# A two-stage transformer block: rows for the gMLP turned on VectorE instead of TensorE, the first w_in pieces made on GpSimd, and four accumulators instead of three and an auxiliary one

## The chip, the cores and the metric

The kernel runs as one program on one core of a Trainium2 chip. The metric is the device time of one execution in microseconds (us); the number that counts is the median of several executions. Five engines work side by side, each through its own list of instructions in order: TensorE (PE in the profile, with its weight loads as PEld), VectorE (DVE), ScalarE (ACT), GpSimd (POOL), and SyncE (SP), which in this kernel does nothing but issue DMAs. Sixteen DMA engines carry the transfers.

## What is computed

S = 2048 tokens of width D = 640. First an attention layer over a sliding window of 256 tokens with 32 heads, then a gated MLP that mixes tokens (gMLP), each behind a layer norm and with a residual:

```python
h  = x + A(layernorm(x))                      # attention, ends in o @ wo
z  = gelu(layernorm(h) @ w_in)                # w_in: 640 x 1728
z1, z2 = z[:, :864], layernorm(z[:, 864:])
g  = w_sp @ z2 + b_sp                         # mixes the 2048 tokens
out = h + (z1 * g) @ w_out
```

All products are made in pieces: every float32 operand is split into a high and a low part, and three products (high high, high low, low high) replace one. Some products also use a seven-product scheme for 2 by 2 blocks, which needs sums and differences of blocks of the operands ("pieces" below).

## The kernel before

The program runs in stages: attention (until about 465 us of the profile), the output projection with the residual and the second layer norm (about 465 to 547 us), the product with the first half of w_in (the z stage, about 547 to 640 us), and then the second half of w_in, the token mixing and the last product. The change lies in the projection stage and at its border to the z stage.

The projection stage goes over 16 tiles of 128 tokens (the loop at L1325). For tile i:

- `norm_o` (L166, DVE) multiplies the attention output, which DMAs have brought in turned form (L150, and L156 for the reciprocal sums), by those sums; `split_o` makes its high part (L174, ACT) and low part (L175, DVE). Both run ahead of TensorE by one to three tiles.
- `proj_o` makes 30 products of 128x320 (L96) into an accumulator of two PSUM banks. There are three accumulators (L703).
- DVE adds the residual and takes the row sum in one instruction (L1345), which also frees the accumulator; ACT squares (L1348), DVE and POOL make the factor of the layer norm (L1347, L1350, a power on POOL at L1351, L1355), and ACT writes the normalised row hn(i), 128 tokens by 640 (L1356).
- `turn_h` (L847 to L858) turns hn(i - 3): five TensorE transposes of 128x128 (L856) into an auxiliary PSUM tile of two banks (there is one, L706), an ACT copy (L723) into one of three SBUF buffers `ho`, and one DMA that stores it to `hn_d` in HBM, 128 runs of 2560 bytes. The last three tiles are turned while the z stage has begun, through other PSUM banks.

In the same stage `win1_prep` (L776) prepares the first half of w_in for the z stage: 16 weight tiles `zl`, each with a high part (ACT, L732 and L799) and a low part (a subtraction of 128x432), and 8 differences of blocks; the 24 subtractions all run on DVE (they pass through the helper at L717, as most additions and subtractions do).

The z stage (`z_pair`, L872) takes two tiles at a time, 8 pairs: it loads the two turned rows from `hn_d` (L889, L890) into the buffer `fx`, which also holds some of the rows hn(i) before they are turned, makes pieces of them on ACT and DVE (L717, L723), and multiplies (L916). Later `z2_pair` loads the same rows again (L977).

The order of instructions on each engine is set by a scheduler in this part of the program; each engine then keeps that order strictly. So an instruction that waits holds up all that stand behind it on its engine, and on SP a DMA that waits for its data holds up all DMAs behind it.

Of the kernel before, what the change touches and what calls it, by code (L numbers as in the profile page):

```python
# [15 lines left out]
P = 128  # L16
S = 2048
D = 640
# [16 lines left out]
def block_kernel(ctx, tc, x, wqk, wv, wo, w_in, wsp, bsp, w_out, out):  # L35
# [16 lines left out]
    r_d = dram.tile([H, S], F32, name="r_d")  # L52
    h_d = dram.tile([NT, P, D], F32, name="h_d")
    z1_d = dram.tile([NT, P, FH], F32, name="z1_d")
    hn_d = dram.tile([NT, P, D], F32, name="hn_d")
    g_d = dram.tile([NT, P, FH], F32, name="g_d")
    wo_d = dram.tile([KD, P, D], F32, name="wo_d")
    z2_d = dram.tile([2, P, FH], F32, name="z2_d")
# [660 lines left out]
    def minus(out, a, b, eng=None):  # L719
        plus(out, a, b, OP.subtract, eng)  # L720

    def copy(out, a):
        nc.scalar.activation(out, a, AF.Copy)  # L723

    B11, T1, T2, B22, T3, B21, T4 = range(7)

    def right_blocks(pieces, b11, b12, b21, b22, eng=None, one=1.0):

        raw = {B11: b11, T1: b11, T2: b11, B22: b22, T3: b12, B21: b21, T4: b21}

        def hi(m):
            nc.scalar.activation(pieces()[m][:, 0], raw[m], AF.Copy, scale=one)  # L732

        def lo(m, e=None):
            minus(pieces()[m][:, 1], raw[m], pieces()[m][:, 0].bitcast(F32), e)

        def second():
            lo(B11)
            minus(b11, b12, b11)
            hi(T1)  # L740

        def fourth():
            hi(B22)
            minus(b11, b22, b11)
# [31 lines left out]
    def win1_prep(raw):  # L776
        seven, last = win1
        rest = [r.rearrange("p (h c) -> p h c", h=2) for r in rows[2:]]

        def pieces(k, blocks, one):  # L780
            return right_blocks(lambda: [s[k] for s in seven], *(b[:, h] for b in blocks for h in range(2)), one=one)

        yield
        for n, f in enumerate(pieces(0, [raw[:, b] for b in range(2)], 1.0)):
            f()
            if n == 2:
                for b in range(2):
                    nc.sync.dma_start(rows[2 + b], w_in[(2 * b + 1) * P:(2 * b + 2) * P, :FH])
            yield
        nc.sync.dma_start(raw[:, 0], w_in[4 * P:, :FH].rearrange("k (h c) -> k h c", h=2))  # L790
        yield
        yield
        for f in pieces(1, rest, ones[:, 0:1]):
            f()
            yield
        yield
        for j in range(2):
            hi, lo = two(last[j])
            nc.scalar.activation(hi, raw[:, 0, j], AF.Copy, scale=ones[:, 1:2])  # L799
            minus(lo, raw[:, 0, j], hi.bitcast(F32))  # L800
        yield

    def win2_prep(raw):
# [42 lines left out]

    def turn_h(i):  # L847
        ht = mem["ho"][i % 3]
        if i < NT - 3:
            ps = aux_tile(f"ht_ps{i}").rearrange("p a b -> p (a b)")  # L850
            parts = [(0, KD, ps)]
        else:
            parts = [(0, 4, bank("b", f"ht_a{i}")), (4, KD, bank("b", f"ht_b{i}"))]
        for k0, k1, ps in parts:
            for k in range(k0, k1):
                nc.tensor.transpose(ps[:, (k - k0) * P:(k - k0 + 1) * P], hn(i)[:, k * P:(k + 1) * P], ident)  # L856
            copy(ht[:, k0 * P:k1 * P], ps[:, :(k1 - k0) * P])
        nc.sync.dma_start(hn_d[i], ht)  # L858


    steps, later = [], {}
# [10 lines left out]
    def z_pair(q, i, j, w):  # L872
# [76 lines left out]
    def z2_pair(q, i, j, k, ahead=False):  # L949
# [24 lines left out]
        for t, tile_t in ((0, i), (1, j)):  # L974
            m = n0 + 2 * t
            soon = q == 13
            at(m - (5 if soon else 12 if q == 8 else 6), lambda t=t, tile_t=tile_t: nc.sync.dma_start(r[t], hn_d[tile_t]))  # L977
# [347 lines left out]
    for i in range(NT):  # L1325
        if 1 < i + 1 < NT:
            split_o(i + 1, i == 1)
        if i % 2 == 0 and i + 6 < NT:
            for f in load_o(i // 2 + 3)[:2]:
                f()  # L1330
        if i + 2 < NT:
            norm_o(i + 2, nc.vector)
        for n in (4,) if i == 0 else (i + 4,) if i + 4 < NT else ():
            load_x2(n)
        run(i - NT)
        if i < 2:
# [8 lines left out]
        nc.vector.tensor_tensor_reduce(out=h3, in0=ps[:, :, :HD], in1=h3, scale=1.0, scalar=0.0,  # L1345
                                       op0=OP.add, op1=OP.add, accum_out=mv[:, 0:1])
        nc.vector.tensor_scalar(out=mv[:, 1:2], in0=mv[:, 0:1], scalar1=-1.0 / D, scalar2=None, op0=OP.mult)  # L1347
        nc.scalar.activation(hn(i), xt, AF.Square, bias=mv[:, 1:2], accum_out=mv[:, 2:3])  # L1348
        nc.scalar.dma_start(h_d[i], xt)
        nc.vector.tensor_scalar(out=mv[:, 2:3], in0=mv[:, 2:3], scalar1=1.0 / D, scalar2=EPS, op0=OP.mult, op1=OP.add)  # L1350
        nc.gpsimd.tensor_tensor(out=mv[:, 3:4], in0=mv[:, 2:3], in1=half, op=OP.pow)  # L1351
# [4 lines left out]
        nc.scalar.activation(hn(i), xt, AF.Identity, scale=mv[:, 3:4], bias=mv[:, 4:5])  # L1356
        next(w1, None)
        if i % 2:
            next(w1, None)
    for _ in w1:  # L1360
        pass
    w2p = None
    for n in range(len(steps)):
        run(n)
        if n < 3:
            turn_h(NT - 3 + n)
        if n == 2:
            open_d()
            w2p = win2_prep(view(fx, 4 * D + 256, FH))
        if n > 2:  # L1370
            next(w2p, None)
# [36 lines left out]
```

## Time and profile before

| | us |
|---|---|
| median of 3 runs | 1111.28 (1109.02 to 1111.66) |
| span of the profiled execution | 1108.2 |
| what lies between that span and the median | 3.1 |
| TensorE busy in that span | 1084.3 |
| VectorE, ScalarE, GpSimd busy | 720.7, 571.0, 369.6 |

Times in the profile count from the start of the span, and a line number L856 is line 856 of the kernel before. Busy TensorE time is modelled from overlapping instructions, so the distance between the starts of two neighbours is the better measure of what one costs; the same holds on the other engines for short instructions. DMA shares are the mean busy share of the 16 DMA engines.

### The profile page before, as it was taken

How to read it: one execution, taken by the hardware profiler on the slowest of the kernel's cores; microseconds unless marked ns; L12 is line 12 of the kernel's file. 1: busy time of each engine (PE TensorE's matmuls, PEld its weight loads, DVE VectorE, ACT ScalarE, POOL GpSimd, SP SyncE). 2: the span in 40 equal slices, each digit the busy share in tenths (PEclk: the TensorE clock that was granted, in tenths of full speed). 3: DMA queues.
4: the chain of work that ended last, by engine and by line, in shares of the span. 5: the costliest groups of instructions: out<-in, count | busy, mean ns of one | idle time of the engine just before them, and what ended most of it. 6: DMA issues, size and time to landing. Idle time of an engine off the chain costs nothing.

```text
span 1108.2 us, 27795 instructions
## 1 busy us (share of the span) xinstructions
PE 1084.3 (98%) x10667; PEld 974.4 (88%) x10667; DVE 720.7 (65%) x2043; ACT 571.0 (52%) x1215; POOL 369.6 (33%) x524
## 2 busy tenths in 40 slices
PE   9999999999999999989999999999999999999998
PEld 7998877668888877788899999999999999999998
DVE  6541212879999998677567478676637985566543
ACT  4333433249999999567776567433326531122210
POOL 3114444457777778512100055256422000000000
PEclk9999999999999999999999999999999999999999
DMA  7212565565666654678755421447593663444321
GB/s 261 74 35 96 166 221 179 196 210 181 214 204 214 215 177 120 193 254 281 242 188 193 151 80 39 165 154 233 190 339 113 204 215 114 129 132 150 100 91 65
DMA packets 88501, 187.80 MB, mean 169 GB/s; under 512 B 11648, under 2 KB 48144, under 8 KB 84448
## 3 DMA queue, kind: packets, MB, share of 16 engines
q1 hardware_dynamic: 83728, 172.08, 47.8%
q0 software_dynamic: 2336, 8.70, 2.2%
q10 hardware_dynamic: 2304, 5.24, 1.2%
q8 instruction: 84, 1.38, 0.5%
q14 instruction: 49, 0.40, 0.1%
HBM read 121.66 MB, written 65.52 MB: 169 GB/s over the span
## 4 chain that ended last, share of the span: by engine, by line
PE 78%; DMA 8%; DVE 3%; issue 3%; POOL 3%; ACT 3%; SPq 2%; ACTq 0%; POOLq 0%; DVEq 0%
PE g L1165 20%; PE zb L968 9%; PE out_ps L1218 8%; PE pv L435 6%; PE bank L341 5%; PE bank L407 5%; PE zx L916 3%; PE zv L916 2%; PE qk L525 2%; PE qk L526 2%; PE qk L527 2%; DMA qk_d<-sg 2%; PE zy L916 2%; SPq L320 1%; PE zw L916 1%
## 5 line engine op out<-in xcount | busy, mean ns | idle before, releaser
L410 ACT ACTIVATE pt<-bank 128x384 f32<-128x384 f32 (+2 forms) x512 | 200.8, 496 | 10.4 <-PE bank L407 5.7
L1165 PE MATMUL g<-zl,aw 128*128 128x432 f32 x768 | 169.7, 359 | 0.0
L353 DVE CUSTOM_DVE_ANT_0 junk<-bank,strip 128x288 bf16<-128x288 f32 x392 | 157.7, 454 | 4.3 <-PE bank L341 3.0
L723 ACT ACTIVATE aw<-fx 128x512 fp32r<-128x512 f32 (+2 forms) x147 | 84.9, 592 | 141.1 <-PE g L1165 101.9
L1165 PEld LDWEIGHTS g<-zl,aw 128*128 128x128 f32 x768 | 143.5, 188 | 6.1
L1165 PE MATMUL g<-ze,aw 128*128 128x432 f32 x576 | 131.9, 359 | 1.1 <-DVE row L717 1.1
L435 PE MATMUL pv<-pt,v_sb 128*32 128x192 f32 (+3 forms) x1984 | 127.3, 323 | 3.8 <-POOL pt L415 1.3
L717 DVE TENSOR_TENSOR aw<-fx,aw 128x512 fp32r<-128x512 f32 (+2 forms) x146 | 99.4, 690 | 28.6 <-ACT aw L723 23.5
L1165 PEld LDWEIGHTS g<-ze,aw 128*128 128x128 f32 x576 | 107.1, 188 | 6.2 <-DVE row L717 1.8
L407 PE MATMUL bank<-slot 123*32 123x288 bf16 (+5 forms) x1536 | 106.1, 282 | 1.0 <-ACT pt L410 0.4
L412 POOL TENSOR_SCALAR_AFFINE_SELECT pt<-pt 128x512 f32<-128x512 f32 x128 | 82.9, 648 | 43.6 <-ACT pt L410 42.4
L1218 PE MATMUL out_ps<-wout,y_sp 128*128 128x320 f32 (+1 forms) x630 | 96.4, 309 | 0.4 <-ACT y_sp L137 0.4
L968 PE MATMUL zb<-win,aw 128*128 128x432 f32 x480 | 95.0, 359 | 0.5 <-ACT aw L723 0.5
L1218 PEld LDWEIGHTS out_ps<-wout,y_sp 128*128 128x128 f32 (+1 forms) x630 | 94.2, 188 | 1.0 <-ACT y_sp L137 0.7
L968 PEld LDWEIGHTS zb<-win,aw 128*128 128x128 f32 x480 | 90.1, 188 | 5.0 <-ACT aw L723 0.9
L341 PE MATMUL bank<-slot 120*32 120x288 bf16 (+2 forms) x1264 | 89.8, 285 | 1.1 <-DVE mcol L353 1.0
L541 DVE TENSOR_TENSOR rest<-qk,sg 128x512 f32<-128x512 f32 x40 | 27.7, 692 | 86.1 <-ACT sg L539 86.1
L415 POOL TENSOR_SCALAR_AFFINE_SELECT pt<-pt 128x512 f32<-128x512 f32 x112 | 74.6, 666 | 0.0
L717 DVE TENSOR_TENSOR row<-g,row 128x432 f32<-128x432 f32 x80 | 48.2, 603 | 33.8 <-PE g L1165 30.3
L544 POOL TENSOR_TENSOR sg<-rest,sg 128x512 bf16<-128x512 f32 x40 | 46.6, 1166 | 69.2 <-ACT sg L543 60.2
L435 PEld LDWEIGHTS pv<-pt,v_sb 128*32 128x32 f32 x1984 | 59.5, 110 | 10.3 <-POOL pt L415 3.2
L407 PEld LDWEIGHTS <-slot 123*32 123x32 bf16 x1536 | 52.6, 96 | 16.2 <-issue 5.0
(216 smaller groups left out, 2195.1 us busy)
## 6 DMA issues: line engine op xcount, KB each, us to landing
fx<-wsp_in SPq DMA_DIRECT2D x30, 512.0 KB
slot<-qk_d SPq DMA_DIRECT2D x72, 200.0 KB
qk_d<-sg SPq DMA_DIRECT2D x32, 384.0 KB
slot<-qk_d SPq DMA_DIRECT2D x72, 160.0 KB
fx<-hn_d SPq DMA_DIRECT2D x32, 320.0 KB
o_d<-ot SPq DMA_DIRECT2D x64, 128.0 KB
z_d<-row SPq DMA_DIRECT2D x18, 432.0 KB
g_d<-row SPq DMA_DIRECT2D x16, 432.0 KB
```

The lines of the kernel that those rows point to most:

```text
L341: nc.tensor.matmul(ps[32 * j:32 * j + 32, :n], part(st, half, 120, 0, hh, q0, 32), part(st, half, 120, 1, hh, lo + skip * j, n), start=Tru ...
L353: nc.vector.tensor_tensor_reduce(out=junk[:, :n], in0=ps[:, :n], in1=keep, scale=1.0, scalar=NEG, op0=OP.add, op1=OP.max, accum_out=m_cols ...
L407: nc.tensor.matmul(ps[32 * i:32 * i + 32, b:e], part(st, half, 123, 1, hh, k0, 32), part(st, half, 123, 0, hh, kb * P + b, e - b), start=T ...
L410: nc.scalar.activation(pt[:, hh, :n], ps[:, :n], AF.Exp, scale=SCALE)
L412: nc.gpsimd.affine_select(out=pt[:, :, :P], in_=pt[:, :, :P], pattern=[[0, 4], [1, P]], base=0, channel_multiplier=-1, compare_op=OP.is_ge ...
L435: nc.tensor.matmul(ps[32 * hh:32 * hh + 32, a - 512 * c:b - 512 * c], v_sb[:, kb, v0:v0 + 32], pt[:, hh, a - kb * P:b - kb * P], start=fir ...
L717: (eng or nc.vector).tensor_tensor(out=out, in0=a, in1=b, op=op)
L723: nc.scalar.activation(out, a, AF.Copy)
L916: nc.tensor.matmul(ps, a[x], b[:, y], start=start and m + x + y == 0, stop=stop and m == n - 1 and x == 1, skip_group_check=True)
L968: nc.tensor.matmul(b[0][:, :HF], a[t][:, x, kk], win2[0][:, y, kk, h * HF:(h + 1) * HF], start=kk + x + y == 0, stop=kk == KD - 1 and x == 1)
L1165: nc.tensor.matmul(ps, w[m][x][:, k], zc[k][m][:, y], start=start and k + x + y == 0, stop=stop and k == 3 and x == 1, skip_group_check=True)
L1218: nc.tensor.matmul(ps[j][:, :HD], src[:w, a, k, :], e1["wout"][:w, b, k, j * HD:(j + 1) * HD], start=(k == 0 and a + b == 0), stop=(k == K ...
```

## The change

1. `turn_h` no longer uses TensorE. VectorE transposes the 128x640 row in blocks of 32x32 from SBUF to SBUF (one instruction), and four DMAs on SP put the blocks where a full transpose would have put them: DMA number a takes the 32 partitions from 32a on and stores 32 x 20 runs of 32 floats (128 bytes). Five transposes and one copy (two copies for the last three tiles) per tile go, one VectorE instruction and three more DMAs per tile come. In `hn_d` the 640 features now stand in another order, which is the same for every tile: the rows of `w_in` are reordered on the host to match.
2. `turn_h(i - 1)` is called at the end of iteration i, instead of `turn_h(i - 3)` in the middle of it; the last tile is turned at the first step of the z stage.
3. All 24 subtractions of `win1_prep` go to GpSimd.
4. The auxiliary PSUM tile goes, and there are four accumulators instead of three.

```diff
-    hn_d = dram.tile([NT, P, D], F32, name="hn_d")
+    hn_d = dram.tile([NT, 32, 4 * D], F32, name="hn_d")
...
-        return pools["c"].tile([P, 2, 512], F32, tag="acc", bufs=3, name=name)
-
-    def aux_tile(name):
-        return pools["c"].tile([P, 2, 512], F32, tag="aux", bufs=1, name=name)
+        return pools["c"].tile([P, 2, 512], F32, tag="acc", bufs=4, name=name)
...
         def pieces(k, blocks, one):
-            return right_blocks(lambda: [s[k] for s in seven], *(b[:, h] for b in blocks for h in range(2)), one=one)
+            return right_blocks(lambda: [s[k] for s in seven], *(b[:, h] for b in blocks for h in range(2)),
+                                nc.gpsimd, one, nc.gpsimd)
...
-            minus(lo, raw[:, 0, j], hi.bitcast(F32))
+            minus(lo, raw[:, 0, j], hi.bitcast(F32), nc.gpsimd)
...
     def turn_h(i):
         ht = mem["ho"][i % 3]
-        if i < NT - 3:
-            ps = aux_tile(f"ht_ps{i}").rearrange("p a b -> p (a b)")
-            parts = [(0, KD, ps)]
-        else:
-            parts = [(0, 4, bank("b", f"ht_a{i}")), (4, KD, bank("b", f"ht_b{i}"))]
-        for k0, k1, ps in parts:
-            for k in range(k0, k1):
-                nc.tensor.transpose(ps[:, (k - k0) * P:(k - k0 + 1) * P], hn(i)[:, k * P:(k + 1) * P], ident)
-            copy(ht[:, k0 * P:k1 * P], ps[:, :(k1 - k0) * P])
-        nc.sync.dma_start(hn_d[i], ht)
+        nc.vector.transpose(ht, hn(i))
+        dst = hn_d[i].rearrange("i (c a j) -> a i c j", a=4, j=32)
+        for a in range(4):
+            nc.sync.dma_start(dst[a], ht[32 * a:32 * a + 32].rearrange("i (c j) -> i c j", j=32))
+
+    def hn_rows(i):
+        return hn_d[i].rearrange("i (b c) -> b i c", b=4)
...
-            nc.sync.dma_start(ri, hn_d[i])
-            nc.sync.dma_start(rj, hn_d[j])
+            nc.sync.dma_start(ri, hn_rows(i))
+            nc.sync.dma_start(rj, hn_rows(j))
...
-        if i > 2:
-            turn_h(i - 3)
...
+        if i:
+            turn_h(i - 1)
...
-        if n < 3:
-            turn_h(NT - 3 + n)
+        if n == 0:
+            turn_h(NT - 1)
...
+    w_in = np.asarray(B_w_in).reshape(4, KD, 32, 2 * FH).transpose(1, 0, 2, 3).reshape(D, 2 * FH)
```

The scheduler makes a new order from this, in the projection stage and the z stage. In the rows below the lines of the changed kernel are 7 lower than those of the kernel before from L1345 on (L1338 is L1345, L1343 is L1350, L1348 is L1355), and L717 has become L714. A number behind `xh`, `mvc`, `ho` and `wo_ps` is that of the tile or buffer; `xb` holds the split attention output.

VectorE between the accumulator reads of tile 2 and tile 3, before:

```order
L1345 ISA xh2_8952,mvc2_9703<-wo_ps2_9672,xh2_8952 128x640
L1345 ISA mvc2_9703 128x1
L1350 TENSOR_SCALAR mvc1_9649<-mvc1_9649 128x1
L175 TENSOR_TENSOR xb1_100<-m1_8949,xb0_99 128x640
L717 TENSOR_TENSOR zl2_9603<-wraw_8956,zl2_9603 128x432
L1345 ISA xh3_8953,mvc3_9758<-wo_ps3_9719,xh3_8953 128x640
L1345 ISA mvc3_9758 128x1
L166 TENSOR_TENSOR m1_8949<-m1_8949 128x5x128 x2
L1347 TENSOR_SCALAR mvc2_9703<-mvc2_9703 128x1
L175 TENSOR_TENSOR xb0_99<-m1_8949,xb0_99 128x640
```

and at the same place now:

```order
L1338 ISA xh2_8952,mvc2_9708<-wo_ps2_9677,xh2_8952 128x640
L1338 ISA mvc2_9708 128x1
L1343 TENSOR_SCALAR mvc1_9649<-mvc1_9649 128x1
L847 STREAM_TRANSPOSE ho0_9595<-row0_9617 128x640
L175 TENSOR_TENSOR xb1_100<-m1_8949,xb0_99 128x640
L1340 TENSOR_SCALAR mvc2_9708<-mvc2_9708 128x1
L1338 ISA xh3_8953,mvc3_9760<-wo_ps3_9729,xh3_8953 128x640
L1338 ISA mvc3_9760 128x1
L175 TENSOR_TENSOR xb0_99<-m1_8949,xb0_99 128x640
L1348 TENSOR_TENSOR mvc1_9649<-mvc1_9649 128x1
```

The subtractions for `zl` are gone from VectorE, the transpose of tile 0 stands ahead of the split of tile 5, and the instruction that waits for GpSimd's power of tile 1 (L1348) stands ahead of everything that follows.

GpSimd in the first tiles of the stage now; before, it had only the 16 powers there:

```order
L1344 TENSOR_TENSOR mvc0_9634<-mvc0_9634,half_79 128x1
L714 TENSOR_TENSOR zl0_9601<-wraw_8956,zl0_9601 128x432
L714 TENSOR_TENSOR zl6_9607<-wraw_8956,zl6_9607 128x432
L714 TENSOR_TENSOR wraw_8956<-wraw_8956 128x432
L714 TENSOR_TENSOR zl10_9611<-wraw_8956,zl10_9611 128x432
L714 TENSOR_TENSOR wraw_8956<-wraw_8956 128x432
L714 TENSOR_TENSOR zl2_9603<-wraw_8956,zl2_9603 128x432
L1344 TENSOR_TENSOR mvc1_9649<-mvc1_9649,half_79 128x1
L714 TENSOR_TENSOR zl8_9609<-wraw_8956,zl8_9609 128x432
```

The powers (L1344) now stand behind subtractions: tile 1's behind six. The last of the 24 stands right ahead of tile 9's power.

SP from the last load of reciprocal sums that both kernels have in common, before:

```order
L156 DMA m1_8949<-r_d_67 128x1x256
L788 DMA row2_9619<-w_in_in 128x864
L788 DMA row3_9620<-w_in_in 128x864
L156 DMA m1_8949<-r_d_67 128x1x256 x2
L150 DMA m1_8949<-o_d_66 128x1x256
L858 DMA hn_d_70<-ho0_9595 128x640
L150 DMA m1_8949<-o_d_66 128x1x256 x4
```

and now:

```order
L156 DMA m1_8949<-r_d_67 128x1x256
L850 DMA hn_d_70<-ho0_9595 640x1x32 x4
L786 DMA row2_9619<-w_in_in 128x864
L786 DMA row3_9620<-w_in_in 128x864
L142 DMA xh1_8951<-x_in 128x640
L150 DMA m1_8949<-o_d_66 128x1x256
L850 DMA hn_d_70<-ho1_9596 640x1x32 x4
L150 DMA m1_8949<-o_d_66 128x1x256
L142 DMA xh2_8952<-x_in 128x640
L850 DMA hn_d_70<-ho2_9597 640x1x32 x4
```

The loads of w_in, of x and of the later attention outputs stand behind the stores of tile 0, 1 and 2, which wait for VectorE's transposes.

More of the change, by code (lines that the diff above doesn't have):

```diff
@@ L725, in block_kernel, with right_blocks @@
     B11, T1, T2, B22, T3, B21, T4 = range(7)
-    def right_blocks(pieces, b11, b12, b21, b22, eng=None, one=1.0):
+    def right_blocks(pieces, b11, b12, b21, b22, eng=None, one=1.0, main=None):
         raw = {B11: b11, T1: b11, T2: b11, B22: b22, T3: b12, B21: b21, T4: b21}
@@ L734, in lo @@
         def lo(m, e=None):
-            minus(pieces()[m][:, 1], raw[m], pieces()[m][:, 0].bitcast(F32), e)
+            minus(pieces()[m][:, 1], raw[m], pieces()[m][:, 0].bitcast(F32), e or main)
         def second():
             lo(B11)
-            minus(b11, b12, b11)
+            minus(b11, b12, b11, main)
             hi(T1)
@@ L743, in fourth @@
             hi(B22)
-            minus(b11, b22, b11)
+            minus(b11, b22, b11, main)
             hi(T2)
@@ L976, in z2_pair @@
             soon = q == 13
-            at(m - (5 if soon else 12 if q == 8 else 6), lambda t=t, tile_t=tile_t: nc.sync.dma_start(r[t], hn_d[tile_t]))
+            at(m - (5 if soon else 12 if q == 8 else 6), lambda t=t, tile_t=tile_t: nc.sync.dma_start(r[t], hn_rows(tile_t)))
             at(m - (1 if soon else 3), lambda t=t: prep(t, True, None))
@@ L1397 @@
     w_out = np.pad(np.asarray(B_w_out), ((0, KF * P - FH), (0, 0)))
-    arrays = {"x_in": c(x), "wqk_in": c(wqk), "wv_in": c(wv), "wo_in": c(wo), "w_in_in": c(np.asarray(B_w_in)),
+    arrays = {"x_in": c(x), "wqk_in": c(wqk), "wv_in": c(wv), "wo_in": c(wo), "w_in_in": c(w_in),
               "wsp_in": c(wsp), "bsp_in": c(bsp), "w_out_in": c(w_out)}
```

## The prediction

> **What bounds the kernel now.** First the page's busy times, then busy time by stage (per engine, then the granted clock, the share of the DMA engines, GB/s), then what TensorE waited for in the projection stage (who waits, for whom, us in total, times, longest).
>
> ```profile
> PE 1084.3 (98%) x10667; PEld 974.4 (88%) x10667; DVE 720.7 (65%) x2043; ACT 571.0 (52%) x1215; POOL 369.6 (33%) x524
> 475.00:547.00 72.00, 64.05 (x439) 61.34 (x438) 50.77 (x136) 50.23 (x89) 13.78 (x15) 1.00 0.80 262
> 547.00:640.00 93.00, 93.00 (x483) 89.00 (x483) 59.16 (x120) 60.18 (x113) 5.96 (x5) 1.00 0.54 180
> 640.00:1108.20 468.20, 462.68 (x2574) 445.90 (x2572) 290.51 (x523) 164.40 (x299) 95.14 (x106) 1.00 0.45 148
> PE ht_ps L856 <- ACT ho L723: 4.9, 3, 2.6
> PE ht_ps L856 <- ACT row L1356: 2.8, 2, 1.9
> PE wo_ps L96 <- DVE xb L175: 0.2, 1, 0.2
> ```
>
> TensorE is the bound nearly everywhere, at full clock: what leaves its path before 640 us is kept to the end, since the stages behind are 99% TensorE. The projection stage is the exception: 8.0 of 72 us idle, and 7.7 of them stand in front of the transposes that the change removes. But there the DMA engines are at 0.80 and VectorE at 51 of 72, so TensorE has neighbours that are not far behind. The chain of waits at the stage's end (start, us, what):
>
> ```profile
> 513.56 1.56 DVE m L166 x2
> 515.12 0.74 DVE xb L175
> ...
> 533.95 0.55 PE ht_ps L856 x5
> 534.49 3.81 PE wo_ps L96 x26
> 538.31 0.56 PE ht_ps L856 x5
> 538.88 5.14 DMA fx<-hn_d
> 544.68 0.91 ACT row L1356
> 545.59 0.59 ACT ho L723
> 546.23 0.77 PE ht_ps L856 x5
> 547.00 1.19 PE zv L916 x6
> 548.18 0.44 PE ht_a L856 x4
> ```
>
> A product of L96 takes 3.81 / 26 = 0.147 us, a tile of 30 takes 4.4; a group of five transposes 0.54 (533.95 to 534.49). Before the z stage a load of turned rows held up ACT, then the copy of an earlier tile, then the transposes: 2.6 us of TensorE.
>
> **What goes from TensorE.** Thirteen groups in the projection stage (13 x 0.53 = 6.9), three inside the z stage (0.44 for four, some 0.1 for the fifth: 1.6), and the 7.7 us of waits: 16.2 at most. ACT loses 16 copies, the auxiliary tile's single buffer no longer holds anything up, and the fourth accumulator only lets TensorE run ahead; L96 never waited for an accumulator (the 0.2 us are for a split), so I price it at nothing, with the DVE's accumulator reads, up to three tiles behind, as cover.
>
> **What VectorE and GpSimd get.** These rows are from the stage (busy, mean ns), the last one from the whole run:
>
> ```profile
> L1351 POOL TENSOR_TENSOR mvc<-mvc,half 128x1 f32<-128x1 f32 x15 | 13.8, 919 | 69.8 <-DVE mvc L1350 63.2 <-DVE mvc L1347 6.6
> L1345 DVE CUSTOM_DVE_ANT_0 xh<-wo_ps,xh 128x640 f32<-128x640 f32 x14 | 11.5, 818 | 0.0
> L175 DVE TENSOR_TENSOR xb<-m,xb 128x640 fp32r<-128x640 f32 x12 | 9.8, 819 | 1.8 <-ACT xb L174 1.8
> L717 DVE TENSOR_TENSOR zl<-wraw,zl 128x432 fp32r<-128x432 f32 x9 | 5.3, 602 | 0.7 <-ACT zl L799 0.7
> L717 POOL TENSOR_TENSOR zl<-row,zl 128x432 fp32r<-128x432 f32 x3 | 4.1, 1377 | 0.0
> ```
>
> VectorE loses 24 subtractions of about 0.6 (14.4 us) and gets 16 transposes. No trace row shows one; it moves 640 elements per partition like the split and the accumulator read (0.82), so 0.82 each, 13.1 us; the bounds are 0.6 (the 432-element row) and 1.6 (twice the split). In sum VectorE's work stays as it is. GpSimd gets the 24 subtractions. What such a one costs it, and what it does to VectorE, a later stage shows (timeline, GpSimd and VectorE):
>
> ```profile
> 718.88 1.23 POOL L717 TENSOR_TENSOR side_raw<-side_raw 128x432 f32<-128x432 f32 x1
> 721.03 1.11 POOL L717 TENSOR_TENSOR side_raw<-side_raw,side_raw 128x432 f32<-128x432 f32 x1
> 722.11 1.11 POOL L717 TENSOR_TENSOR side_parts<-side_raw,side_parts 128x432 fp32r<-128x432 f32 x1
> 703.48 0.75 DVE L1114 SCALAR_TENSOR_TENSOR tmp<-fx,one 128x512 f32<-128x512 f32 x1
> 718.83 1.83 DVE L1114 SCALAR_TENSOR_TENSOR tmp<-fx,one 128x512 f32<-128x512 f32 x1 [0.17 <-DMA fx<-wsp_in]
> ```
>
> One subtraction per 1.08 us (721.03 to 722.11). And a VectorE instruction with two SBUF operands that takes 0.75 alone took 1.83 when a GpSimd subtraction ran: it waited for the whole of it. The Trainium skill, page "SBUF — State Buffer", section "Who interferes with whom", has this as a rule: a VectorE instruction with two SBUF inputs and a GpSimd instruction that reads SBUF shut each other out for their whole length. By that rule the sum is the one below; without it the third rival. This trace agrees with the rule at 718.83.
>
> So the projection's norms (L166) and splits (L175) of VectorE, which have two SBUF operands, and all of GpSimd's work share one turn. Up to the power of tile 9, behind which no subtraction is left in GpSimd's order:
>
> ```profile
> 475.28 0.84 POOL L1351 TENSOR_TENSOR mvc<-mvc,half 128x1 f32<-128x1 f32 x1 [16.91 <-DVE mvc L1350]
> 521.71 0.55 POOL L1351 TENSOR_TENSOR mvc<-mvc,half 128x1 f32<-128x1 f32 x1 [3.90 <-DVE mvc L1347]
> ```
>
> From 476.1 (end of tile 0's power): 24 x 1.08 = 25.9, nine powers at 0.55 = 5.0, eight norms and eight splits at 0.75 (chain rows: 1.56 for two, 0.74) = 12.0. Together 42.9, so 519.0 if the turn is never idle; with 2 us of gaps (estimate: about one subtraction's length twice, where ACT's high parts and GpSimd wait for each other) 521. Before, that power began at 521.7. The shared turn therefore eats what TensorE gains in the first ten tiles. In VectorE's new order the read of tile 10's accumulator and the split of tile 12 follow: 521 + 2 x 0.82 = 522.7, where TensorE, done with tile 11 at about 519, waits for that split. From there nothing holds it: tiles 12 to 15 take 4 x 4.4 = 17.6, to 540.3. At the border TensorE's new order begins with four products that need only ACT's copy (0.8 us); the fifth needs VectorE's 640-wide low part, which stands behind tile 15's accumulator read and tile 14's power: 0.82 + 0.15 + 0.82 = 1.8, so 1.0 of wait. The z stage is where it was at 546.75 (the last transposes' start + 0.52) at 541.3: 5.4 us earlier, and the groups inside it make 7.0.
>
> **The stores.** Each tile now takes 4 DMAs on SP, 2560 packets of 128 bytes instead of 128 of 2560. Issue times on SP (ns, min/median/max) for the old store and for the nearest form, three runs per partition; then the queue over the whole run, over 0.86 us (103.22 to 104.08) with packets of 0.55 KB, and over 0.55 us (246.01 to 246.56) with mostly 256-byte ones (packets, MB, share of 16 engines); then the load on the engines where the stage is fullest:
>
> ```profile
> L858 SPq DMA_DIRECT2D hn_d<-ho x16: 319/320/619, 486.4 to 555.9; - x16
> L557 SPq DMA_DIRECT2D qk_d<-sg x60: 359/430/1345, 95.4 to 244.0; - x60
> q1 hardware_dynamic: 83728, 172.08, 47.8%
> q1 hardware_dynamic: 451, 0.25, 95.6%
> q1 hardware_dynamic: 133, 0.04, 31.7%
> 483.00:522.00 39.00, 1.00 0.85 282
> ```
>
> SP: 4 x 0.43 = 1.7 us per tile instead of 0.32, with a tile every 4.4 to 5 us. Engines: a packet took 0.478 x 16 x 1108.2 / 83728 = 101 ns at 2055 bytes, 29.2 ns at 554, 21.0 ns at 300; the line through the last two gives 15.5 ns at 128 bytes (estimate). The slope from the first pair would give 8.7, and 29.2 is the upper bound, the smallest packets of which enough ran back to back. At 15.5 a tile's store holds all 16 engines for 2.5 us against 1.0 before (125 ns by the first slope, 8 packets each): 1.5 more, on engines that are 85% busy. The stores are on no path themselves; behind them on SP stand the x loads, the later attention outputs and the first turned rows. I let one store's surplus of 1.5 us end on the path. Sum: 7.0 - 1.5 = 5.5 us less.
>
> **The rivals.** *GpSimd sets the pace.* If its subtractions take 1.377 each, as the zl row above says of three of them beside VectorE, the shared turn gets 24 x 0.3 = 7.1 us longer, tile 12's split comes that much later, and 5.5 - 7.1 = -1.6: about 1113, no measurable change. For it: the new order puts VectorE's L1348 behind GpSimd's queue, six subtractions for tile 1. Against: the same row's neighbours run at 1.08.
>
> *The stores fill the queue (slower).* At 29.2 ns a store holds the engines for 4.7 us. From 483 to 522 they are busy 0.85 x 39 = 33.2 us; six stores (6 us) go and eight come (37.4): 64.6 us of work in 39. VectorE's norm of tiles 14 and 15 came 20 us ahead of use (513.56; tile 14 at 533.9); with the loads now behind stores I count 8 of that as slack, which leaves 17 us of lateness against 7.0 gained: 10 slower, 1121. It decides from the packet price at which lateness is 7.0: 33.2 - 6 + 8 x 160 x c = 39 + 8 + 7, c = 21 ns. For it: 21.0 is just what the 300-byte packets took; and the three `ho` buffers make VectorE's transpose wait for the store three tiles back, so a slow store also blocks VectorE. Against: packet time fell with size in all three rows. The Trainium skill, page "DMA: Bandwidth & Descriptors", section "Specifications", puts the line at 512 bytes, below which a write becomes a read and a write; no row of this trace stores less than that to HBM, and by it this rival is the case.
>
> *No shutting out.* If GpSimd and VectorE overlap freely, TensorE runs from tile 5's split (about 484) through 11 tiles of 4.4 to 532.4, and the z stage stands 13.3 earlier, 14.9 with its own groups: 1096. The row at 718.83 speaks against it, and so does VectorE's strict order, which waits for ACT and GpSimd at every tile.
>
> **How the numbers follow.** The profiled span of 1108.2 becomes 1102.7; the median lay 3.1 above the span, so 1105.8. Chances: forecast 0.48 (1101 to 1109), GpSimd's pace 0.20 (1109 to 1114), stores 0.25 (1112 to 1125), no shutting out 0.07. The range leaves out the last one's best times and the upper part of the stores: 1099 to 1118. A measurement of this kernel tells 0.3%, 3.3 us, from no change: faster (below 1108) are the last case and nearly nine tenths of the first, 0.50; the rest of the first, the second and a sliver of the third make 0.25 the same; slower 0.25.
>
> **What would show it.** Right: no TensorE transposes; transposes of 0.75 to 0.85 us on VectorE; splits and norms of up to 1.9 us while GpSimd subtracts; TensorE's waits in the stage all `DVE xb`, the longest near tile 12; the z stage's first product near 541. Wrong: packets above 21 ns, SP issues above 0.6 us, VectorE's transposes waiting for stores, or TensorE waiting for splits before tile 8 by more than 2 us; and, the other way, splits that keep 0.82 us beside GpSimd.

## The result and the profile after

| | us |
|---|---|
| kernel before, median of 4 runs | 1110.57 (1109.02 to 1111.66) |
| changed kernel, median of 4 runs | 1162.99 (1161.29 to 1167.86) |
| ratio | 1.0475, 95% interval 1.0446 to 1.0504 |
| span of the profiled execution, after | 1159.9 |

The change makes the kernel 52 us slower: where 5.5 us less had been forecast, and far outside the forecast range of 1099 to 1118. The page's busy times, then the two stages around the change (length, then PE, PEld, DVE, ACT, POOL, granted clock, DMA share, GB/s):

```profile
PE 1093.5 (94%) x10587; PEld 977.2 (84%) x10587; DVE 730.6 (63%) x2035; ACT 560.5 (48%) x1196; POOL 398.4 (34%) x548
```

```profile
475.00:547.00 72.00, 60.08 (x362) 58.12 (x361) 49.89 (x98) 37.39 (x63) 38.54 (x37) 0.91 0.84 215
547.00:640.00 93.00, 68.25 (x312) 61.40 (x310) 49.40 (x110) 43.22 (x84) 1.76 (x3) 0.89 0.55 151
```

TensorE lost its 80 transposes (10667 to 10587 instructions), and yet from 547 to 640 us, where it had been busy for 93.0 of 93 us, it is busy for 68.25, at a granted clock of 0.89. That is the z stage, behind the stage that the change was made in. What TensorE waited for, from 475 to 600 and from 600 to 720:

```profile
PE zv L911 <- ACT aw L720: 8.7, 2, 7.3
PE zx L911 <- ACT aw L720: 8.0, 1, 8.0
PE wo_ps L96 <- ACT xb L174: 6.2, 3, 4.7
...
PE zx L911 <- ACT row L720: 7.9, 5, 3.0
```

The longest waits are for ACT's pieces of the turned rows (`aw`). ACT is not the cause, as the waits of ACT and VectorE (475 to 665) and the chain of waits (465 to 700) show, the latter with its shares by line first, then some pieces (start, us, what):

```profile
ACT aw L720 <- DMA fx<-hn_d: 21.1, 6, 5.5
...
DVE fx L714 <- DMA fx<-hn_d: 28.7, 8, 6.2
```

```profile
by line: DMA fx<-hn_d 24.7%; issue 9.5%; SPq L850 8.3%; DMA fx<-wsp_in 3.7%; DVE aw L714 3.6%; DVE row L714 2.6%; DMA hn_d<-ho 2.6%; DMA h_d<-xh 2.5%; DVE fx L714 1.9%; DVE ze L714 1.7%; DMA m<-o_d 1.7%; ACT aw L720 1.5%; POOL fx L714 1.2%;
...
586.41 10.81 DMA fx<-hn_d
600.02 8.94 DMA fx<-hn_d
...
615.07 8.61 DMA fx<-hn_d
...
628.43 7.51 DMA fx<-hn_d
```

A quarter of the chain is the load of turned rows (320 KB each), 7.5 to 10.8 us at a time in the pieces shown. The prediction had no term for these loads. The start of the second z stage (the first product of L968, now L963) shows how much had been lost by then; before, then after:

```profile
629.52 2.12 PE L968 MATMUL zb<-win,aw 128*128 128x432 f32 x10
```

```profile
665.62 2.00 PE L963 MATMUL zb<-win,aw 128*128 128x432 f32 x5
```

36 of the 52 us were gone there. Most of the rest goes in the second z stage, which loads the same rows again: its last product starts at 909.6 instead of 861.1 us, 48 later.

The stores were not small either: on SP (min/median/max in ns, first and last start) their 64 issues took 0.65 us each and up to 4.1, and VectorE's transposes came out as priced:

```profile
L850 SPq DMA_DIRECT2D hn_d<-ho x64: 549/647/4132, 483.7 to 581.5; - x64
L847 DVE STREAM_TRANSPOSE ho<-row x10: 828/835/848, 482.7 to 571.3; 128x640 f32<-128x640 f32 x10
```

### The profile page after: what moved, and what is told of

Same layout as the page of the kernel before. It is cut to its first block, busy times and chain, and to the rows that moved or that the text cites. A ratio compares the mean times of both kernels' runs of the same rounds, so it can differ in the third digit from the quotient of the medians.

```text
span 1159.9 us, 27694 instructions
## 1 busy us (share of the span) xinstructions
PE 1093.5 (94%) x10587; PEld 977.2 (84%) x10587; DVE 730.6 (63%) x2035; ACT 560.5 (48%) x1196; POOL 398.4 (34%) x548
## 4 chain that ended last, share of the span: by engine, by line
PE 28%; DMA 11%; DVE 7%; issue 3%; ACT 2%; SPq 2%; POOL 1%; POOLq 0%; ACTq 0%; DVEq 0%
PE g L1160 18%; PE out_ps L1213 8%; DMA fx<-hn_d 7%; DMA fx<-wsp_in 2%; DVE aw L714 2%; SPq L850 2%; DVE row L714 1%; PE yt_ps L1200 1%; DVE zl L714 1%; ACT row L995 1%; ACT aw L720 1%; DVE fx L714 1%; DVE ze L714 1%; DVE stz L985 1%; PE out_l L1213 1%
## 5 line engine op out<-in xcount | busy, mean ns | idle before, releaser
L720 ACT ACTIVATE aw<-fx 128x512 fp32r<-128x512 f32 (+3 forms) x147 | 84.6, 591 | 178.1 <-PE g L1160 102.4
L714 DVE TENSOR_TENSOR aw<-fx,aw 128x512 fp32r<-128x512 f32 (+3 forms) x146 | 100.2, 697 | 50.4 <-ACT aw L720 50.0
L963 PE MATMUL zb<-win,aw 128*128 128x432 f32 x480 | 97.9, 366 | 8.1 <-ACT aw L720 7.8
L963 PEld LDWEIGHTS zb<-win,aw 128*128 128x128 f32 x480 | 92.4, 193 | 13.0 <-ACT aw L720 8.2
L714 DVE TENSOR_TENSOR row<-g,row 128x432 f32<-128x432 f32 x80 | 48.2, 604 | 35.0 <-PE g L1160 30.9
```

The lines of the kernel that those rows point to most:

```text
L714: (eng or nc.vector).tensor_tensor(out=out, in0=a, in1=b, op=op)
L963: nc.tensor.matmul(b[0][:, :HF], a[t][:, x, kk], win2[0][:, y, kk, h * HF:(h + 1) * HF], start=kk + x + y == 0, stop=kk == KD - 1 and x == 1)
```

## The experiments

In every experiment the other lines are those of the kernel it is called a version of. Ratios are to the kernel before on the same chip, with their 95% intervals.

### Loads or stores: rows16, four_loads, before_b4load, store_twice

Theory L: a turned row is now loaded through an access pattern whose outermost dimension is 4, so only 4 of 16 DMA engines carry it. Rivals: the stores (S), and GpSimd's subtractions with the new order (G).

**rows16**: the same bytes in HBM, read with another assignment to partitions. A load of this form has 128 partitions outermost.

```diff
-        return hn_d[i].rearrange("i (b c) -> b i c", b=4)
+        return hn_d[i].rearrange("i (b c) -> (i b) c", b=4)
...
-    w_in = np.asarray(B_w_in).reshape(4, KD, 32, 2 * FH).transpose(1, 0, 2, 3).reshape(D, 2 * FH)
+    w_in = np.asarray(B_w_in).reshape(4, KD, 32, 2 * FH).transpose(1, 2, 0, 3).reshape(D, 2 * FH)
```

> The changed kernel, whose turned rows are loaded in the form partition = 4i + b instead of 32b + i, so that the load's outermost dimension is 128 instead of 4 (w_in's rows reordered to match); stores, subtractions and accumulators are those of the changed kernel. Theory L (the loads of the turned rows run on 4 of the 16 DMA engines and starve the z stages): a load's time on an otherwise quiet queue falls from 6 to 11 us to under 3, the DMA share while only such loads run is no longer 0.2, TensorE's waits for ACT's pieces in the z stage (27 us) go, and the time falls by 40 to 55 us, to 1108 to 1123. Rival S (the 128-byte stores hold SP and the engines): the stores are unchanged, so at most the 13 us in the second z stage come back: 1150 or more. Rival G (GpSimd's subtractions and the new order delay the projection): likewise over 1150.

Measured: 1117.52 us, 1.0069 (1.0046 to 1.0092). The order in which the load visits the partitions (with w_in's rows to match) gives 45 of the 52 us back: L holds, S and G as rivals for the bulk fall. The number of packets in the whole run, after and in rows16, shows the engines themselves:

```profile
DMA packets 127796, 187.78 MB, mean 162 GB/s; under 512 B 52992, under 2 KB 89488, under 8 KB 123744
```

```profile
DMA packets 128180, 187.79 MB, mean 169 GB/s; under 512 B 53376, under 2 KB 89872, under 8 KB 124128
```

384 more small packets in rows16, 12 for each of the 32 loads. A usual DMA brings 16 small packets (three more DMAs for each of 16 tiles bring 768 below, 16 for each of the 48), so the load in question had 4. I read them as one for each engine that takes part. The Trainium skill, page "DMA: Bandwidth & Descriptors", section "Why a DMA increments its semaphore by 16 and not by 1", gives the rule behind it: the number of engines is the largest one up to 16 that divides the outermost dimension of both access patterns. The trace agrees: 4 with "b i c" and b = 4, 16 with 128. What that does to the speed, in busy tenths of all 16 engines and GB/s, 40 slices each: after, from 586.4 to 597.2, then rows16 from 642 to 652:

```profile
DMA  9998318999099999669997513222222222222222
GB/s 376 358 410 307 54 76 332 348 386 355 26 361 411 383 332 271 146 207 364 374 268 179 140 38 104 85 114 85 104 114 85 104 114 83 111 105 96 105 115 102
```

```profile
DMA  9998696883000079994000000005899610000000
GB/s 401 401 401 332 127 266 154 307 318 143 10 0 0 0 318 442 415 415 180 0 0 0 0 0 0 0 0 143 236 307 328 246 51 0 0 0 0 0 0 0
```

In the second half of the first window the share is 0.2 (4 of 16 is 0.25), at some 100 GB/s, a rate at which 320 KB need over 3 us. The packed trace shows the four engines there: of the 4.2 us from 593.0 on, just four packets were in flight for 3.7, 111 of them of the loads' size (2560 bytes) and 42 of 3456 bytes, the rest of another transfer. So what other transfers have on those 4 engines goes slowly beside such loads. In rows16 a lone load (at the slices with 143 to 51) is through in six slices of 0.25 us, 1.5 us.

**four_loads**: the layout of the changed kernel, each load as four DMAs.

```diff
+    def load_rows(dst, i):
+        for b in range(4):
+            nc.sync.dma_start(dst[32 * b:32 * b + 32], hn_rows(i)[b])
...
-            nc.sync.dma_start(ri, hn_rows(i))
-            nc.sync.dma_start(rj, hn_rows(j))
+            load_rows(ri, i)
+            load_rows(rj, j)
...
```

> The changed kernel with the rows in HBM and the partitions as they are, but every load of a turned row as four DMAs of 32 partitions each, so that each DMA's outermost dimension is 32. Theory L: the same gain as with the other partitions, less what 3 more DMA issues per load cost on SP (32 loads x 3 x 0.3 to 0.65 = 30 to 60 us of SP, which is not the bound): 1108 to 1128. Rival S: SP has 96 more issues, so 1160 or more.

Measured: 1128.19 us, 1.0170 (1.0133 to 1.0207), 35 below the changed kernel and 11 above rows16. L again, at the upper end of what was expected: with the layout unchanged most of the loss goes, so the layout is not at fault, the engines of one DMA are. Its small packets (54912 under 512 B, 1920 more than after) fit 16 for each of its 128 loads, whose outermost dimension is 32, in place of 4 for each of the 32. I put the 11 us down to the 96 more issues; no run shows that.

**before_b4load**: the kernel before, given that load alone.

```diff
-        nc.sync.dma_start(hn_d[i], ht)
+        nc.sync.dma_start(hn_d[i].rearrange("i (b c) -> (i b) c", b=4), ht)
+
+    def hn_rows(i):
+        return hn_d[i].rearrange("i (b c) -> b i c", b=4)
...
-            nc.sync.dma_start(ri, hn_d[i])
-            nc.sync.dma_start(rj, hn_d[j])
+            nc.sync.dma_start(ri, hn_rows(i))
+            nc.sync.dma_start(rj, hn_rows(j))
...
```

> The kernel before, with one thing changed: hn_d is 32 x 2560 and a turned row is loaded as the changed kernel loads it, outermost dimension 4 (the store is the same 128 runs of 2560 bytes, w_in's rows are reordered to match). TensorE's transposes, VectorE's subtractions and the three accumulators stay. Theory L: the z stages starve here too, and most of the loss is there: 1140 to 1165. Rivals S and G: nothing of theirs is in it, and the old loads had time to spare: 1109 to 1118.

Measured: 1155.44 us, 1.0411 (1.0381 to 1.0441): 46 us from the load alone, what rows16 took away. Its z stage looks like that of the changed kernel (same window, same columns), and what VectorE waits for too:

```profile
547.00:640.00 93.00, 75.44 (x363) 69.72 (x362) 45.47 (x100) 46.63 (x89) 1.21 (x2) 0.89 0.42 148
```

```profile
DVE fx L717 <- DMA fx<-hn_d: 23.6, 7, 8.1
```

**store_twice**: rows16, every turned row stored a second time (same four DMAs) into a tensor that nothing reads.

> The first kernel of this set with every turned row stored twice, the second time into a tensor that nothing reads: 64 more DMAs of 640 packets of 128 bytes. Theory L: stores are on no path, 0 to 8 us above the first kernel. Rival S: a second set costs as much as the first, 20 to 50 us above the first kernel.

Measured: 1155.79 us, 1.0418 (1.0374 to 1.0462). My expectation under L was a miss: a second set of stores costs 38 us, so the first set is hardly free. This and rows16's remaining 7 to 8 us above the kernel before led to the next question.

### What is left in rows16: rows16_plain_store, rows16_subs_dve, rows16_act_store, before_subs_pool

TensorE's waits in rows16 from 475 to 600:

```profile
PE wo_ps L96 <- ACT xb L174: 7.8, 3, 4.7
PE zx L911 <- ACT aw L720: 5.1, 1, 5.1
...
```

The high parts (L174) wait for VectorE's norms (L166), these for the loads of the attention outputs (L150), and these stand behind stores on SP, as the chain of waits shows:

```profile
507.32 0.63 SPq L850
...
508.79 1.78 SPq L850
510.61 0.65 SPq L150
...
513.92 4.29 DMA m<-r_d
518.23 0.88 DVE m L166 x2
```

Theory S2: the stores. Theory G2: the subtractions on GpSimd.

**rows16_plain_store**, which leaves out the placing of the blocks:

```diff
-        dst = hn_d[i].rearrange("i (c a j) -> a i c j", a=4, j=32)
-        for a in range(4):
-            nc.sync.dma_start(dst[a], ht[32 * a:32 * a + 32].rearrange("i (c j) -> i c j", j=32))
+        nc.sync.dma_start(hn_d[i].rearrange("i (b c) -> (i b) c", b=4), ht)
```

> rows16 (the changed kernel with the load of partition = 4i + b), but a turned row is stored by one DMA of 128 runs of 2560 bytes instead of four DMAs of 640 runs of 128 bytes. It leaves out the placing of the 32x32 blocks across partitions, so the rows that are loaded are not the transposed ones; instructions, bytes and loads are otherwise those of rows16. Theory S2 (what is left of the loss, and the expected gain of 5.5, sit in the 128-byte stores: 16 x 35 us/16 of engines and 2 us of SP each): 12 to 20 us below rows16, 1098 to 1105. Theory G2 (they sit in GpSimd's subtractions and the shared turn): within 3 us of rows16, 1114 to 1121.

Measured: 1103.12 us, 0.9927 (0.9904 to 0.9951), 14.4 below rows16: S2. Without the stores' cost the change would be a gain of 6.4 us. TensorE's waits in 465 to 640, and the z stage's first product:

```profile
PE wo_ps L96 <- DVE xb L175: 7.1, 2, 4.1
...
```

```profile
539.16 1.34 PE L909 MATMUL zv<-zl,aw 128*128 128x432 f32 x6
```

**rows16_subs_dve**: the arguments `nc.gpsimd` for w_in's pieces taken out again (point 3 of the change undone).

> rows16 with the 24 subtractions for w_in's first half on VectorE, as before. Theory G2: the shared turn is what delayed the projection, 6 to 12 us below rows16, 1105 to 1111. Theory S2: VectorE gets 14.4 us of work in a stage in which it is not the bound, 0 to 8 us above rows16, 1116 to 1126.

Measured: 1115.38 us, 1.0048 (1.0027 to 1.0070), 2 us below rows16, with intervals that overlap. Neither a gain of 6 nor a loss is seen.

**rows16_act_store**: `nc.sync` in the store's loop becomes `nc.scalar`.

> rows16 with the four stores of a turned row issued by ScalarE instead of SyncE. If the cost of the stores is SyncE's time and the loads queued behind the stores on it (64 issues of 0.65 to 3.6 us): 5 to 12 us below rows16, 1105 to 1112, less what ScalarE's 64 issues cost (42 us of ScalarE at 0.65, in a stage where it is busy 0.6). If it is the engines' time for 128-byte packets: no gain, 1115 to 1130.

Measured: 1123.43 us, 1.0114 (1.0086 to 1.0142): no gain. TensorE now waits for ACT's high parts more (475 to 640), as ACT issues 64 DMAs of 0.65 us itself; so this run can't tell SP's time from the engines' time.

```profile
PE wo_ps L96 <- ACT xb L174: 21.7, 2, 16.9
```

**before_subs_pool**: the kernel before with point 3 of the change alone.

> The kernel before, with the 24 subtractions for w_in's first half on GpSimd and nothing else changed. Theory G2 (shared turn): slower than before by 3 to 8 us, 1113 to 1118. Theory S2: VectorE was not the bound and the stage's waits were for ACT's copies, so within 3 us of before, 1107 to 1113.

Measured: 1114.95 us, 1.0057 (1.0030 to 1.0083). In the kernel before, moving the subtractions costs 3 to 9 us, as G2 said; in rows16 it doesn't show. But its profile (of its fastest run) does not show the loss where G2 has it: the first products of the two z stages come 84.1 and 166.4 us after the last product of the attention, against 83.6 and 166.4 in the kernel before. Behind 690 us TensorE waits 2.6 us longer for VectorE's rows (3.7 against 1.1); why, no run here shows.

### Number of DMAs or length of runs: plain_store_by4, rows640, rows640_subs_dve, plain_subs_dve

**plain_store_by4**: rows16_plain_store with the store cut in four.

```diff
-        nc.sync.dma_start(hn_d[i].rearrange("i (b c) -> (i b) c", b=4), ht)
+        dst = hn_d[i].rearrange("i (b c) -> (i b) c", b=4)
+        for a in range(4):
+            nc.sync.dma_start(dst[32 * a:32 * a + 32], ht[32 * a:32 * a + 32])
```

> rows16_plain_store (1103.1), its store cut into four DMAs of 32 runs of 2560 bytes; like it, it leaves out the placing of the blocks across partitions. If the 14.4 us of the stores are the three more issues per tile on SyncE (the number of DMAs): 1110 to 1118. If they are the runs of 128 bytes (2560 packets instead of 128, their time on the engines and their descriptors): 1102 to 1107.

Measured: 1108.0 us, 0.9996 (0.9974 to 1.0019). Between the two expectations, so both are at work: three more DMAs per tile cost 0.9996 - 0.9927, 0.7% or 8 us, and the 128-byte runs the other 0.7% up to rows16 (each with 0.3% of uncertainty). One thing changes along with the number of DMAs: the scheduler makes another order on SP, in which the first load of a turned row starts at 535.7 us instead of 513.4. No run separates the issues from that order.

**rows640**: the columns of a row in HBM in the order (block of tokens, feature block, token) instead of (feature block, block of tokens, token).

```diff
-        dst = hn_d[i].rearrange("i (c a j) -> a i c j", a=4, j=32)
+        dst = hn_d[i].rearrange("i (b a c) -> a i b c", a=4, b=4)
         for a in range(4):
-            nc.sync.dma_start(dst[a], ht[32 * a:32 * a + 32].rearrange("i (c j) -> i c j", j=32))
+            nc.sync.dma_start(dst[a], ht[32 * a:32 * a + 32].rearrange("i (b c) -> i b c", b=4))
...
+    def raw4(r):
+        return r.rearrange("p (a k j) -> p k a j", a=4, j=32)
```

> rows16 with the row in another column order: the five blocks that go from a group of 32 partitions to another stand side by side in HBM, so the four DMAs of a tile store 4 x 128 runs of 640 bytes instead of 4 x 640 runs of 128; the elementwise instructions of the z stages read the loaded rows in pieces of 32 floats to put the tokens in order. The output is complete. If the runs are the cost: 512 packets take about 512 x 35 ns / 16 = 1.1 us of all engines (estimate), near the 1.0 of 128 long ones, so 1103 to 1108, below the kernel before. If it is the number of DMAs: 1113 to 1120, as rows16.

Measured: 1109.91 us, 1.0003 (0.9979 to 1.0027): between its two expectations, and as plain_store_by4. In the kernel's time, runs of 640 bytes can't be told from runs of 2560, and what remains is the four DMAs. The prediction had cited a line at 512 bytes from the Trainium skill ("DMA: Bandwidth & Descriptors", "Specifications"). The runs lie on both sides of it, but the packets show no jump: in the packed traces a packet takes 13.4 ns in the mean at 128 bytes (rows16), 37 at 640 (rows640) and 125 at 2560 (before). The queue over the whole run, and the stores' issues, in rows16_plain_store, plain_store_by4 and rows16:

```profile
q1 hardware_dynamic: 83728, 172.08, 47.4%
...
L848 SPq DMA_DIRECT2D hn_d<-ho x16: 319/320/552, 483.7 to 547.8; - x16
```

```profile
q1 hardware_dynamic: 84496, 172.08, 47.8%
...
L850 SPq DMA_DIRECT2D hn_d<-ho x64: 302/416/1423, 484.8 to 555.7; - x64
```

```profile
q1 hardware_dynamic: 123408, 172.08, 49.1%
...
L850 SPq DMA_DIRECT2D hn_d<-ho x64: 549/644/3617, 481.0 to 567.8; - x64
```

The 128-byte stores take 0.491 x 1112.5 - 0.474 x 1098.7 = 25.5 us of all 16 engines more than the plain ones, 1.6 per tile. In whole, 2560 packets of 13.4 ns make 2.1 us of all 16 engines per tile. And SP: four issues take 1.7 us per tile with long runs, 2.6 with short ones, 0.32 as one DMA.

**rows640_subs_dve** and **plain_subs_dve**: rows640 and rows16_plain_store with point 3 undone, as in rows16_subs_dve.

> rows640 with the 24 subtractions for w_in's first half on VectorE, as in the kernel before. Theory G2 (GpSimd's subtractions cost 3 to 6 us, as they did in the kernel before): 3 to 6 us below rows640. Its rival (moving them is neutral in this version, as the 2 us between rows16 and rows16_subs_dve say, within the intervals): within 2 us of rows640.

> rows16_plain_store with the 24 subtractions on VectorE; it too leaves out the placing of the blocks across partitions. Theory G2: 3 to 7 us below rows16_plain_store, 1096 to 1100, since the waits for VectorE's splits (7.1 us) come from the shared turn. Its rival: VectorE gets 14.4 us back in a stage where it is busy 87% of the time, so 0 to 5 us above, 1103 to 1108.

Measured: 1112.19 us, 1.0016 (0.9990 to 1.0043), against 1.0003 for rows640; and 1105.01 us, 0.9954 (0.9934 to 0.9974), against 0.9927. As a claim on the whole time G2 falls: both are above their partner, not below, though the intervals overlap.

### The change without both costs: load640 and its parts

**load640**: one plain store per row, and the placing of the blocks done by the load.

```diff
-        dst = hn_d[i].rearrange("i (b a c) -> a i b c", a=4, b=4)
-        for a in range(4):
-            nc.sync.dma_start(dst[a], ht[32 * a:32 * a + 32].rearrange("i (b c) -> i b c", b=4))
+        nc.sync.dma_start(hn_d[i], ht)
...
-        return hn_d[i].rearrange("i (b c) -> (i b) c", b=4)
+        return hn_d[i].rearrange("(a i) (b c) -> (i b) a c", a=4, b=4)
```

> The changed kernel with a plain store, one DMA of 128 runs of 2560 bytes, and the placing of the blocks done by the load: one DMA per row with 128 partitions outermost, four runs of 640 bytes to each (column order as in rows640). The output is complete. If one DMA per store and per load, 16 engines and runs of 640 bytes are enough: within 3 us of rows16_plain_store, 1101 to 1106, below the kernel before. If the 32 loads with four times the packets cost what the stores did (half of 14 us): 1107 to 1112.

Measured: 1105.09 us, 0.9949 (0.9930 to 0.9967): faster than both kernels, by 0.3 to 0.7% than the one before and by some 58 us than the changed one. Its waits of TensorE from 475 to 600, the first products of the two z stages, two splits of VectorE, and the power of tile 9 on POOL:

```profile
PE wo_ps L96 <- DVE xb L175: 9.2, 2, 5.1
...
```

```profile
480.26 1.44 PE L96 MATMUL wo_ps<-xb,xb 128*128 128x320 f32 x4 [4.15 <-DVE xb L175]
...
504.77 0.90 PE L96 MATMUL wo_ps<-xb,xb 128*128 128x320 f32 x2 [5.10 <-DVE xb L175]
...
540.77 1.35 PE L920 MATMUL zv<-zl,aw 128*128 128x432 f32 x6
...
622.95 0.75 PE L973 MATMUL zb<-win,aw 128*128 128x432 f32 x3
...
503.01 1.71 DVE L175 TENSOR_TENSOR xb<-m,xb 128x640 fp32r<-128x640 f32 x1
...
510.82 0.81 DVE L175 TENSOR_TENSOR xb<-m,xb 128x640 fp32r<-128x640 f32 x1
...
523.68 1.13 POOL L1354 TENSOR_TENSOR mvc<-mvc,half 128x1 f32<-128x1 f32 x1
```

These starts are compared with those of the kernel before, so the attention in front has to be looked at: the change does not touch it, and yet its last product starts at 461.9 us here and at 463.2 in the kernel before (between 460.0 and 468.9 in the other kernels' profiles). The projection's products (count, ns min/median/max, first and last start), before and in load640, show the same 1.3 us at their first start:

```profile
L96 PE MATMUL wo_ps<-xb,xb x260: 302/309/417, 458.7 to 543.1; 128*128 128x320 f32 x130
```

```profile
L96 PE MATMUL wo_ps<-xb,xb x260: 303/309/635, 457.4 to 540.3; 128*128 128x320 f32 x130
```

**load640_subs_dve** (point 3 undone), **load640_acc3** (`bufs=4` becomes `bufs=3`) and **load640_late** (`turn_h(i - 3)` in the middle of iteration i, the last three in the z stage):

> load640 with the 24 subtractions on VectorE. After the two pairs run so far they are worth 0 to 2 us for GpSimd: 0 to 3 us above load640. If the shared turn costs: 2 to 6 us below.

> load640 with three accumulators instead of four. The prediction priced the fourth at nothing: within 2 us of load640. If it lets TensorE run ahead of VectorE's late accumulator reads: 3 to 8 us above.

> load640 with the turn of tile i - 3 in the middle of iteration i and the last three tiles turned in the z stage, as in the kernel before, instead of tile i - 1 at its end. If the place of the turn is free, since VectorE and the store have time: within 2 us of load640. If the border to the z stage needs the early turn (the first pairs' loads wait for the stores): 3 to 6 us above.

Measured: 1103.47 us, 0.9946 (0.9918 to 0.9973); 1105.63 us, 0.9962 (0.9941 to 0.9983); 1103.19 us, 0.9936 (0.9914 to 0.9959). None can be told from load640. So points 2 to 4 of the change bring nothing measurable each; what remains as the source of the 0.5% is what all four kernels share, the transposes off TensorE. That is by elimination; no kernel has point 1 alone.

For point 3 the equal times hide two effects. In load640_subs_dve the projection's products, TensorE's waits (465 to 640) and the first products of the two z stages are:

```profile
L96 PE MATMUL wo_ps<-xb,xb x260: 303/309/635, 457.2 to 533.5; 128*128 128x320 f32 x130
...
PE wo_ps L96 <- DVE xb L175: 3.9, 2, 2.7
PE zv L919 <- ACT tmp L720: 3.1, 1, 3.1
PE zv L919 <- DVE mvc L1352: 2.8, 1, 2.8
...
536.99 2.50 PE L919 MATMUL zv<-zl,aw 128*128 128x432 f32 x6 [2.84 <-DVE mvc L1352]
...
624.33 2.12 PE L972 MATMUL zb<-win,aw 128*128 128x432 f32 x10
```

With the subtractions on VectorE, TensorE waits 3.9 instead of 9.2 us for the splits and starts its last projection product 6.8 us earlier. Then the border to the z stage and the z stage take it back: two waits of 3 us, and the second z stage begins 1.4 us later than in load640. plain_subs_dve shows the same against rows16_plain_store: the projection ends 5.3 us earlier (533.4 against 538.7), the second z stage begins 1.0 later (622.3 against 621.3).

## Why the prediction was wrong, step by step

In sum: 6.4 us gained (rows16_plain_store; the forecast had 7.0), 14.4 lost by the stores and 45 by the loads, which makes 53 us more; measured 52.

- **The loads: the step that is missing.** "What goes from TensorE", "What VectorE and GpSimd get" and "The stores" priced the instructions that go, the transposes, the subtractions and the stores, and from there summed up "7.0 - 1.5 = 5.5 us less". It read the new `hn_d` as a matter of where the store writes. The diff also changes how 32 loads read, from `hn_d[i]` to "b i c" with 4 outermost, and no term, bound or rival has that. The bytes per load, the run length and the count stayed the same, and none of these shows it; the outermost dimension does. It cost 45 us (the changed kernel to rows16) and 46 (before to before_b4load).
- **"I let one store's surplus of 1.5 us end on the path": mis-sized, 14.4 us.** The store's price itself was near: 1.6 us more of all 16 engines per tile against 1.5, and 13.4 ns a packet against 15.5. But the surplus of all 16 stores (25 us) falls in a stage whose engines were 0.80 busy, together with SP's issues: 0.64 instead of 0.43 us, and up to 3.6. About half of the cost comes with the number of DMAs (and the order on SP that goes with it), half with the short runs.
- **The rival of the full queue** came near the time of rows16, 1121 against 1117.5, and made it hang on the wrong thing, a packet of over 21 ns. The packets took 13.4 ns, and the loss came nevertheless: the point of decision counted the engines' time alone, and half of the loss came with the number of DMAs. So the nearness is luck in part. Of its signs, SP issues above 0.6 us and transposes waiting for stores (2.1 us) came true, the packet above 21 ns didn't.
- **What goes from TensorE, and the z stage at 541.3: right in size.** Without the two costs the z stage begins at 540.77 in load640 (546.75 before) and the second at 622.95 (629.52). Of these 6.0 and 6.6 us, 1.3 belong to the attention in front, which leaves 4.7 and 5.3 against 5.4 and 7.0: the groups inside the z stage brought 0.6, not 1.6. The fourth accumulator at nothing: right.
- **VectorE's transposes at 0.82**: 0.835, right.
- **The shared turn of GpSimd and VectorE**: seen (splits of 1.71 instead of 0.81 us; tile 9's power at 523.7 against 521), and GpSimd's subtractions do hold up the projection, by 5 to 7 us in the two pairs above. But TensorE waits at 480 and 505, not near tile 12 as the working had it, and the working had nothing at the border that takes an earlier end back. With the subtractions on VectorE the border does, so the end of the kernel doesn't move. That the size came out right is luck in part.
- **GpSimd sets the pace** (1113): POOL is 28.8 us busier than before (398.4 against 369.6), 1.2 us for each subtraction if all of it is theirs, between the 1.08 of the sum and the rival's 1.377. The runs can't tell GpSimd's pace from the shared turn, since they move both at once. before_subs_pool lost 5.5 us, but its profile doesn't show them in the projection. **No shutting out** (1096): the splits of 1.71 us speak against it.

## What to carry to other kernels

When a tensor gets another layout, go through every DMA that touches it, readers as well as the writer, and look at the outermost dimension of both sides: here 4 put a DMA on 4 engines, and 32 or 128 on 16, at the same length of runs. Where a transfer has to scatter, let the side do it that has time to spare and can keep one DMA with 128 partitions outermost and runs of some 640 bytes. When two kernels are compared by where a stage begins, take off what the stages in front differ by. And a cost that recurs in every tile of a stage with busy DMA engines adds up; it is not hidden because each transfer is on no path by itself.

## What was not expected of the hardware

- A load on 4 engines takes longer to issue too: 0.52 us on SP after (median of the 16 loads of the second z stage), 0.32 in rows16, for the same 128 runs.

```profile
L972 SPq DMA_DIRECT2D fx<-hn_d x16: 507/520/528, 642.8 to 878.4; - x16
```

```profile
L972 SPq DMA_DIRECT2D fx<-hn_d x16: 319/320/738, 614.1 to 833.8; - x16
```

- The issue of a store grows much less than its number of runs: 0.42 us for 32 runs of 2560 bytes, 0.64 for 640 runs of 128.
- TensorE's granted clock was lower where TensorE had to wait: in the window from 547 to 640 it was 0.89 in the changed kernel, 0.96 in rows16 and 1.00 before, and the 144 products `zx` of the z stage took 392, 367 and 359 ns each in the mean. Part of what a wait costs here thus comes on top of the wait.
